# Four of the ten token-group norms of an adaLN block transposed by the DMA crossbar instead of TensorE

## The chip, the cores and the metric
The kernel runs on one core of one Trainium2 chip. The metric is the device time of one execution in microseconds; the median of ten runs of the kernel before is 248.68 us (247.54 to 251.53). A core has five engines with a queue each: TensorE (PE, matmuls; PEld is its weight load), VectorE (DVE), ScalarE (ACT), GpSimd (POOL) and SyncE (SP), which here only issues DMAs. The profile's lines name them so.

## The reference
One transformer block on 2048 tokens of width 512, in bf16. A conditioning vector gives six rows of 512: a shift, a scale and a gate for each half of the block.

```python
mod = (silu(c) @ w_mod).reshape(1, 6, 1, -1)
sa, ca, ga, sb, cb, gb = (mod[:, i] for i in range(6))
h = layernorm(x) * (1 + ca) + sa
x = x + ga * attention(h, wqkv, wo)       # 32 heads of 16; each token sees 8 keys, 2 apart, backwards
h = layernorm(x) * (1 + cb) + sb
x = x + gb * ((gelu(h @ w_gate) * (h @ w_up)) @ w_down)      # 512 -> 1792 -> 512
```

The attention is a sliding, dilated one: `idx = pos[:, None] - 2 * arange(8)`, and positions before the first token are masked.

## The kernel before
**Groups.** The tokens are worked in five groups (`GROUPS`, L256): groups 0 and 1 of 256 tokens, groups 2, 3 and 4 of 512. Each goes through the same stages, and the loop at L928 emits them: `ln1` (first norm), `emit_qkv`, `emit_attention` (which ends with the second norm), and `emit_ffn` for the group before.

**Norms.** The tokens lie on the partitions when a norm is taken. `norm` (L529) writes (x - mean) * rstd for 128 tokens on VectorE into a tile `xn` of [128 tokens, 2, 512], so a 512-token group has two such tiles (`half` 0 and 1). The matmuls that follow need the 512 features on the partitions. `transposed` (L551) does that: TensorE transposes blocks of 128x128 into PSUM tiles `tp` (16 for a group of 512 tokens), and `modulate` (L545) takes each block row of 128 features from PSUM on ScalarE, multiplies by 1 + scale and adds the shift (both one number per partition there), and writes `hT` (first norm) or `h2T` (second norm), laid out [128, 4 feature blocks `dt`, tokens]. Four modulations make a group.

**Matmuls.** `emit_qkv` (L646) reads `hT[g][:, dt, 0:n]` as the moving operand, `emit_ffn` (L888) reads `h2[g][:, dt, 0:n]`, gate and up in turn (`g_ps`, `u_ps`); four matmuls over `dt` fill one PSUM tile. ScalarE takes the gelu of the gate (L897) and copies up (L900), VectorE multiplies them (L901), and the down projection `y_ps` (L914) is added to x on VectorE (L922) and stored (L925). For the last 128 tokens, the down projection is cut in two column ranges (`cuts`, L905), so that the first part can be added and stored while the second is computed.

**Attention.** Products q times shifted k on VectorE (`pq`, L728) are folded on TensorE (`LT`, L740); a maximum on VectorE, one matmul that subtracts it (L770), exponentials on ScalarE (L777), their sum on TensorE (`ss`, L785), its inverse on ScalarE (L790), products with v on VectorE (`pv`, L806), a fold (`o_ps`, L825) and the output projection (`x_ps`, L850). v goes to DRAM (`scr`, L672) and comes back in a shifted layout (`vR`, L689).

**Order.** No loop order is kept. Every operation is put into a `Plan` with an engine, an estimated time and a priority (`PRI`, smaller goes first). `Plan.order` (L92) is a list scheduler: it takes the operation that can start earliest by these estimates (with an added `MARGIN` for an operation's engine), and the priority decides among equals. A DMA is estimated by its issue time on SP and by its bytes over a bandwidth, plus a fixed latency; `AHEAD` and `SKEW` shape that. The result is one fixed instruction order on each engine. Every engine executes its queue in order, so an instruction that waits holds all behind it on that engine. All DMAs but one small one are issued from SP's queue. The tags in `BUFS` (L196) tell how many buffers each tile has: two for `hT`, `h2T`, `xn1` and `xn2`, and in PSUM four for `psF` and two each for `psL` and `psB`; the `tp` tiles of second norms are in `psB`, those of first norms of groups 1 to 4 in `psF`.

Of the kernel before, what the change touches and what calls it, by code (L numbers as in the profile page):

```python
# [8 lines left out]
ACT = mybir.ActivationFunctionType  # L9
ALU = mybir.AluOpType  # L10
AX = mybir.AxisListType
F32 = mybir.dt.float32
BF16 = mybir.dt.bfloat16
# [171 lines left out]
class Engines:  # L185
    def __init__(self, nc, pl):
# [11 lines left out]
        ("e", 1), ("oT", 1), ("h2T", 2), ("gl", 3), ("ub", 3), ("hh", 8))  # L198
BLOCKS1 = ()
BLOCKS2 = ()  # L200
LNACT = (0, 1)
SECOND = ()
MERGE = (3, 4)
FMERGE = 0
PRI = {
        "mod0": -12.4,
        "ln1": (-1502.5, -1237, -338.7, -29.4, 227.5),
        "qkv": (-71.9, 355.8, 239.3, 407.9, 1355.7),
        "att": (60.2, 400.6, -1102.5, 575.4, 1925.6),
        "ffn": (1146.5, 2723.5, 3129, 2182.7, 1503.5),  # L210
        "glu": (-357.2, 325.4, -1793.4, 205.8, 1599.5),
        "mod": (-117, -108, -507.7),
        "wo": 1499.4,
        "wd": 1669.5,
        "scr": -3244.8,
        "vR": -3579.5,
        "warm": (5, 7, 0, 3),
        "load": {"wv": -995.5, "x1": -998.36, "x2": -989.51, "wm2": -981.48, "wo": -880.76, "x3": -990.01,
        "wm3": -882.56, "wm4": -988.97, "x4": -992.67, "Wg": -867.81, "Wu": -862.75, "wm5": -862.25, "Wd":
        -862.75},  # L220
}
Plan.MARGIN = {"pe": 0.33, "act": 0.29, "dve": 0.21, "pool": 0.16, "sp": -1.5}
Plan.AHEAD = 3.4
Plan.SKEW = 1.21
Plan.TURN = 0
# [3 lines left out]
def kernel(  # L229
# [13 lines left out]
    nc = tc.nc  # L243
    P = 128
# [37 lines left out]
    def act_us(n, ptr=0):  # L282
        return 0.055 + n * 0.833e-3 + 0.093 * ptr
# [267 lines left out]
    def transposed(xns, n, dst, off, p, seq, tags, split, lo=0):  # L551
        per = 2 if n == SG else 4
        for dtp in range(DT // per):
# [16 lines left out]
            for dd in range(per):  # L570
# [6 lines left out]
                else:  # L577
                    modulate(dst, lambda dd=dd, tp=tp: tp[:, dd, 0:n], dt, off, n, p, [tp], lo)

    def ln1(g, dst, p):  # L580
        xns = []
        tok0, n = GROUPS[g]
        for half in range(n // 256):
# [24 lines left out]
            for i in range(2):  # L608
                norm(tok + P * i, xn, i, Mean(mv), rstd, p)
        transposed(xns, n, dst, 0, p, "ln1", ("psL",) if g == 0 else ("psF", "psF"), g == 0)  # L610

# [16 lines left out]
    def emit_qkv(g):  # L628
# [10 lines left out]
        for step, (b, j) in enumerate(order):  # L639
# [3 lines left out]
            def mm(b, j, ps, jls, dts):  # L643
                whole = len(dts) == DT
                for jl, dt in [(jl, dt) for jl in jls for dt in dts]:
                    nc.tensor.matmul(ps[:, jl, :], lhsT=wqkv[b][:, dt, j + jl:D:4], rhs=hT[g][:, dt, 0:n],  # L646
                                     start=(dt == 0 and (jl == 0 or whole)),
                                     stop=(dt == DT - 1 and (jl == nj - 1 or whole)))
# [29 lines left out]
    def emit_attention(g):  # L678
# [155 lines left out]
        lo = tok0 % SG if FMERGE else 0  # L834
        h2[g] = h2[g - 1] if lo else T("h2T", [P, DT, SG], BF16, "h2T")
        xns = []
        for half in range(n // 256):
# [31 lines left out]
            for i in range(2):  # L869
                norm(tok0 + 256 * half + P * i, xn, i, sx, rstd, p2)  # L870
        transposed(xns, n, h2[g], 8, base + 12, "ln2", ("psB", "psB"), False, lo)

    def emit_ffn(g):
# [4 lines left out]
        for u in range(units):  # L878
            p = PRI["ffn"][g] + u
            gu = []  # L880
            for Wt in (Wg, Wu):
                ps = T("psF", [P, nf, n], F32, "g_ps" if Wt is Wg else "u_ps", "ffn")

                def mm(Wt=Wt, ps=ps, u=u):
                    for f in range(nf):
                        ft = u * nf + f
                        for dt in range(DT):
                            nc.tensor.matmul(ps[:, f, :], lhsT=Wt[:, dt, ft * P:(ft + 1) * P],  # L888
                                             rhs=h2[g][:, dt, 0:n], start=(dt == 0), stop=(dt == DT - 1))

# [12 lines left out]
        for c4 in range(n // P):  # L903
            gc = tok0 // P + c4
            cuts = ((0, 256), (256, D)) if gc == S // P - 1 else ((0, D),)  # L905
            for cut, (lo_d, hi_d) in enumerate(cuts):
# [21 lines left out]
    for g in range(NG):  # L928
        hT[g] = T("hT", [P, DT, GROUPS[g][1]], BF16, "hT")
        ln1(g, hT[g], PRI["ln1"][g])  # L930
# [46 lines left out]
```

## Time and profile before

| What | us |
|---|---|
| median of 10 runs | 248.68 (247.54 to 251.53) |
| the profiled execution's own time | 248.26 |
| its span, first to last instruction | 246.2 |
| TensorE busy | 236.9 |
| VectorE busy | 158.6 |
| ScalarE busy | 158.6 |
| 128 transposes on TensorE, their share of busy time | 11.4 |

The page divides the span in 40 slices of 6.2 us and prints the busy share of each engine in each as a digit (9 is 90% or more). Groups of instructions are listed as line, engine, operation, output and inputs, shape, count, then busy time and mean duration in ns, then how long the engine sat idle just before them and what ended that. A matmul's duration is longer than the distance to the next one, since they are pipelined; from a timeline, the distance between starts gives what one costs. In a timeline's line stand start and length in us, then the instructions merged in it.

### The profile page before, as it was taken

What the parts mean: (1) busy time and instruction counts of PE and PEld (TensorE: products, weight loads), DVE (VectorE), ACT (ScalarE), POOL (GpSimd) and SP (SyncE); (2) the same over time, 40 slices, a digit from 0 to 9 for tenths busy, and PEclk for the clock granted to TensorE, in tenths of its full rate; (3) what the DMA queues carried; (4) which work ended last, traced back from release to release, by engine and by line L of the source; (5) the groups of instructions that cost most, each with busy time, mean ns of one, the idle gap of its engine ahead of it and who ended that gap; (6) DMA issues with size and microseconds to landing.
All of it is one profiled execution on the core that took longest, in us unless ns stands there. A gap on an engine that the chain in (4) does not pass through costs nothing.

```text
span 246.2 us, 4292 instructions
## 1 busy us (share of the span) xinstructions
PE 236.9 (96%) x1642; PEld 130.9 (53%) x1666; DVE 158.6 (64%) x302; ACT 158.6 (64%) x293; POOL 19.3 (8%) x37
## 2 busy tenths in 40 slices
PE   7699989999999999999999999999999999999995
PEld 3588545557675547675444444444445444444453
DVE  4589869739998699972699895189464222222222
ACT  5197887989476778568777575655768701666400
POOL 6004330010001000040000002000011000000000
PEclk9999999999999999999999999999999999999999
DMA  5999999998800129500108600001000010100011
GB/s 159 352 356 340 304 271 360 216 315 208 176 0 0 43 70 249 121 0 4 43 18 203 128 0 0 24 21 43 0 4 1 0 42 3 43 0 0 3 43 43
DMA packets 27030, 25.89 MB, mean 105 GB/s; under 512 B 1409, under 2 KB 25858, under 8 KB 27010
## 3 DMA queue, kind: packets, MB, share of 16 engines
q1 hardware_dynamic: 27008, 25.61, 38.8%
q8 instruction: 13, 0.21, 0.4%
q14 instruction: 7, 0.06, 0.1%
q10 hardware_dynamic: 2, 0.00, 0.0%
HBM read 21.40 MB, written 4.21 MB: 104 GB/s over the span
## 4 chain that ended last, share of the span: by engine, by line
PE 79%; DVE 6%; DMA 5%; SPq 3%; ACT 2%; POOL 1%; issue 1%; DVEq 0%; POOLq 0%
PE u_ps L888 20%; PE g_ps L888 20%; PE y_ps L914 19%; PE qkv_ps L646 7%; PE x_ps L850 5%; DMA wm<-in_w_mod_dram 3%; DVE st L592 3%; PE o_ps L825 3%; PE LT L740 2%; DMA wk<-in_A_wqkv_dram 2%; PE tp L560 2%; POOL rstd L536 1%; DVE pq L728 1%; DVE xn L531 1%; SPq L414 1%
## 5 line engine op out<-in xcount | busy, mean ns | idle before, releaser
L888 PE MATMUL g_ps<-h2T,Wg 128*128 128x512 bf16 (+1 forms) x277 | 57.2, 336 | 0.2
L888 PE MATMUL u_ps<-h2T,Wu 128*128 128x512 bf16 (+1 forms) x275 | 57.1, 336 | 0.2
L914 PE MATMUL y_ps<-WdP,hht 128*128 128x512 bf16 (+1 forms) x231 | 50.6, 366 | 0.3
L897 ACT ACTIVATE gl<-g_ps 128x512 bf16<-128x512 f32 x56 | 33.7, 602 | 24.1 <-PE g_ps L888 16.3
L900 ACT CAST ub<-u_ps 128x512 bf16<-128x512 f32 x56 | 32.8, 586 | 17.5 <-PE u_ps L888 16.5
L901 DVE TENSOR_TENSOR hht<-gl,ub 128x512 bf16<-128x512 bf16 x56 | 23.4, 425 | 32.0 <-ACT ub L900 31.4
L888 PEld LDWEIGHTS <-Wu 128*128 128x128 bf16 x280 | 26.9, 98 | 22.4 <-issue 1.9
L888 PEld LDWEIGHTS <-Wg 128*128 128x128 bf16 x280 | 27.2, 98 | 21.4 <-issue 0.4
L728 DVE TENSOR_TENSOR pq<-qT,kT 128x2048 bf16<-128x2048 bf16 x32 | 37.9, 1222 | 0.3 <-ACT kT L668 0.3
L914 PEld LDWEIGHTS <-hht 128*128 128x128 bf16 x238 | 23.1, 98 | 23.9
L922 DVE TENSOR_TENSOR x_sg<-y_ps,x_sg 128x512 bf16<-128x512 f32 (+1 forms) x17 | 10.7, 656 | 28.6 <-PE y_ps L914 28.6
L806 DVE TENSOR_TENSOR pv<-e,vR 128x2048 bf16<-128x2048 bf16 x24 | 28.3, 1222 | 0.1
L536 POOL TENSOR_TENSOR rstd<-rstd,neghalf 128x2 f32<-128x2 f32 x14 | 15.0, 1076 | 166.5 <-DVE rstd L865 107.6
L646 PE MATMUL qkv_ps<-hT,wk 128*128 128x512 bf16 (+1 forms) x76 | 16.1, 335 | 0.8 <-DMA wk<-in_A_wqkv_dram 0.5
L646 PE MATMUL qkv_ps<-hT,wq 128*128 128x512 bf16 (+1 forms) x79 | 16.6, 336 | 0.1
L646 PE MATMUL qkv_ps<-hT,wv 128*128 128x512 bf16 (+1 forms) x80 | 15.7, 337 | 0.0
L850 PE MATMUL x_ps<-woP,oT 128*128 128x512 bf16 x61 | 15.0, 379 | 0.2
L546 ACT ACTIVATE h2T<-tp,modT,scl 128x512 bf16<-128x512 bf16 (+1 forms) x20 | 12.8, 695 | 2.2 <-PE tp L560 2.2
L857 ACT ACTIVATE xn<-x_sg 128x512 bf16<-128x512 bf16 x16 | 10.1, 629 | 4.8 <-DVE x_sg L854 4.5
L668 ACT CAST kT<-qkv_ps 128x512 bf16<-128x512 f32 x16 | 9.4, 589 | 4.6 <-PE qkv_ps L646 4.1
L668 ACT CAST qT<-qkv_ps 128x512 bf16<-128x512 f32 x16 | 9.5, 593 | 4.4 <-PE qkv_ps L646 4.4
L854 DVE SCALAR_TENSOR_TENSOR x_sg<-x_ps,x_sg 128x512 bf16<-128x512 f32 x16 | 10.8, 691 | 1.8 <-PE x_ps L850 1.7
(92 smaller groups left out, 223.1 us busy)
## 6 DMA issues: line engine op xcount, KB each, us to landing
vR<-scr SPq DMA_DIRECT2D x24, 260.0 KB, 5.0
vR<-scr SPq DMA_DIRECT2D x8, 264.0 KB, 9.8
wm<-in_w_mod_dram SPq DMA_DIRECT2D x8, 256.0 KB, 5.5
out_dram<-x_sg SPq DMA_DIRECT2D x15, 128.0 KB, 1.7
Wg<-in_B_w_gate_dram SPq DMA_DIRECT2D x2, 896.0 KB, 9.4
scr<-vT SPq DMA_DIRECT2D x7, 256.0 KB, 6.2
Wu<-in_B_w_up_dram SPq DMA_DIRECT2D x2, 896.0 KB, 12.6
WdP<-in_B_w_down_dram SPq DMA_DIRECT2D x2, 896.0 KB, 8.8
```

What stands on the lines that cost most here:

```text
L536: gp(0.75, lambda: nc.gpsimd.tensor_tensor(out=rstd[:], in0=rstd[:], in1=neghalf[:, 0:2], op=ALU.pow), r=[rstd, neghalf], w=[rstd], pri=p)
L546: act(act_us(n, 2), lambda: nc.scalar.activation(out=dst[:, dt, lo:lo + n], in_=src(), func=ACT.Identity, scale=scl[:, off // 2 + dt:off / ...
L646: nc.tensor.matmul(ps[:, jl, :], lhsT=wqkv[b][:, dt, j + jl:D:4], rhs=hT[g][:, dt, 0:n], start=(dt == 0 and (jl == 0 or whole)), stop=(dt ...
L668: act(act_us(SG), lambda dst=dst, ps=ps: nc.scalar.copy(out=dst(), in_=ps[:]), r=[ps], w=w, pri=p)
L728: dve(1.145, lambda j=j, wg=wg, no=no, t=pq[m]: nc.vector.tensor_tensor(out=t[:], in0=_ap(q[g][:, j, :], [[0, no], [1, n]]), in1=_ap(kT[:, ...
L806: dve(1.145, lambda jj=jj, jl=jl, wg=wg, t=pv[m]: nc.vector.tensor_tensor(out=t[:], in0=_ap(e[:, wg, :], [[0, 4], [1, n]]), in1=vR[g][jj][ ...
L850: nc.tensor.matmul(x1_ps[:], lhsT=oT[:, j, c4 * P:(c4 + 1) * P], rhs=woP[:, j, :], start=(j == 0), stop=(j == 3))
L888: nc.tensor.matmul(ps[:, f, :], lhsT=Wt[:, dt, ft * P:(ft + 1) * P], rhs=h2[g][:, dt, 0:n], start=(dt == 0), stop=(dt == DT - 1))
L897: act(act_us(SG), lambda gl=gl, ps=gu[0]: nc.scalar.activation(out=gl[:], in_=flat(ps), func=ACT.Gelu_apprx_tanh), r=[gu[0]], w=[gl], pri= ...
L900: act(act_us(SG), lambda ub=ub, ps=gu[1]: nc.scalar.copy(out=ub[:], in_=flat(ps)), r=[gu[1]], w=[ub], pri=p)
L901: dve(0.339, lambda gl=gl, ub=ub, ht=hh[u // 2], u=u: nc.vector.tensor_tensor(out=ht[:, u % 2, :], in0=gl[:], in1=ub[:], op=ALU.mult), r=[ ...
L914: nc.tensor.matmul(y_ps[:], lhsT=hh[u // 2][:, u % 2, f * n + c4 * P:f * n + (c4 + 1) * P], rhs=WdP[:, ft, lo_d:hi_d], start=(ft == 0), st ...
```

## The change
The second norms of groups 2, 3 and 4 and the first norm of group 4 no longer use `transposed`. A new helper `crossbar` issues one `dma_start_transpose` from SP for each of a group's two `xn` tiles (256 KB each, SBUF to SBUF), which writes the tile transposed into `hT` or `h2T`. Then four ScalarE instructions scale and shift that tile in place. These tiles are laid out [128, token block, feature block, 128 tokens], so the matmuls read their moving operand in four runs of 128 columns with a stride (`columns`), and write their PSUM tile under the same shape (`shaped`).

All priorities and load priorities are set anew, as are the margins, `AHEAD` and `SKEW`. The last 128 tokens' down projection is cut at column 384 instead of 256.

```diff
-BLOCKS1 = ()
-BLOCKS2 = ()
+CUT = 384
+XB1 = {4: "act"}
+XB2 = {2: "act", 3: "act", 4: "act"}
 PRI = {
-        "mod0": -12.4,
-        "ln1": (-1502.5, -1237, -338.7, -29.4, 227.5),
-        "qkv": (-71.9, 355.8, 239.3, 407.9, 1355.7),
-        "att": (60.2, 400.6, -1102.5, 575.4, 1925.6),
-        "ffn": (1146.5, 2723.5, 3129, 2182.7, 1503.5),
+        "mod0": -90.9,
+        "ln1": (-1628, -1309.8, -689.8, -49.3, 487.8),
+        "qkv": (-615.4, 221.2, 164.3, 607.2, 1344.9),
+        "att": (-458.5, 37.3, -1094.5, 559.4, 1849),
+        "ffn": (1261.5, 2894.6, 2852.9, 2242.7, 1657.1),
...
-        "load": {"wv": -995.5, "x1": -998.36, "x2": -989.51, "wm2": -981.48, "wo": -880.76, "x3": -990.01,
-        "wm3": -882.56, "wm4": -988.97, "x4": -992.67, "Wg": -867.81, "Wu": -862.75, "wm5": -862.25, "Wd":
+        "load": {"wv": -995.5, "x1": -998.36, "x2": -995.23, "wm2": -996.59, "wo": -880.76, "x3": -1009.12,
+        "wm3": -995, "wm4": -996.09, "x4": -995.73, "Wg": -870.11, "Wu": -862.75, "wm5": -860.91, "Wd":
         -862.75},
 }
-Plan.MARGIN = {"pe": 0.33, "act": 0.29, "dve": 0.21, "pool": 0.16, "sp": -1.5}
-Plan.AHEAD = 3.4
-Plan.SKEW = 1.21
+Plan.MARGIN = {"pe": 0.45, "act": 0.17, "dve": 0.22, "pool": 0.29, "sp": -0.46}
+Plan.AHEAD = 2.49
+Plan.SKEW = 2
...
+    def crossbar(xns, n, dst, off, p, on):
+        for half, xn in enumerate(xns):
+            dma(262e3, lambda half=half, xn=xn: nc.sync.dma_start_transpose(
+                out=dst[:, 2 * half:2 * half + 2, :, :].rearrange("p c d t -> p (c d) t"),
+                in_=xn[:].rearrange("p i d -> p (i d)")), r=[xn], w=[(dst, ("half", half))], pri=p, us=1.25, bw=290e3)
+        for dt in range(DT):
...
+                act(act_us(n, 2), lambda dt=dt: nc.scalar.activation(
+                    out=dst[:, :, dt, :], in_=dst[:, :, dt, :], func=ACT.Identity,
+                    scale=scl[:, off // 2 + dt:off // 2 + dt + 1], bias=modT[:, off + dt:off + dt + 1]),
+                    r=[dst, (scl, off), (modT, off)], w=[(dst, dt)], pri=p)
+
+    def columns(t, g, dt, xb):
+        return t[:, :, dt, :] if g in xb else t[:, dt, 0:GROUPS[g][1]]
+
+    def shaped(ap, g, xb):
+        return ap.rearrange("p (c t) -> p c t", t=P) if g in xb else ap
...
-        transposed(xns, n, dst, 0, p, "ln1", ("psL",) if g == 0 else ("psF", "psF"), g == 0)
+        if g in XB1:
+            crossbar(xns, n, dst, 0, p, XB1[g])
+        else:
+            transposed(xns, n, dst, 0, p, "ln1", ("psL",) if g == 0 else ("psF", "psF"), g == 0)
...
-                    nc.tensor.matmul(ps[:, jl, :], lhsT=wqkv[b][:, dt, j + jl:D:4], rhs=hT[g][:, dt, 0:n],
+                    nc.tensor.matmul(shaped(ps[:, jl, :], g, XB1), lhsT=wqkv[b][:, dt, j + jl:D:4],
+                                     rhs=columns(hT[g], g, dt, XB1),
...
-        transposed(xns, n, h2[g], 8, base + 12, "ln2", ("psB", "psB"), False, lo)
+        if g in XB2:
+            crossbar(xns, n, h2[g], 8, base + 12, XB2[g])
+        else:
+            transposed(xns, n, h2[g], 8, base + 12, "ln2", ("psB", "psB"), False, lo)
...
-                            nc.tensor.matmul(ps[:, f, :], lhsT=Wt[:, dt, ft * P:(ft + 1) * P],
-                                             rhs=h2[g][:, dt, 0:n], start=(dt == 0), stop=(dt == DT - 1))
+                            nc.tensor.matmul(shaped(ps[:, f, :], g, XB2), lhsT=Wt[:, dt, ft * P:(ft + 1) * P],
+                                             rhs=columns(h2[g], g, dt, XB2), start=(dt == 0), stop=(dt == DT - 1))
...
-            cuts = ((0, 256), (256, D)) if gc == S // P - 1 else ((0, D),)
+            cuts = ((0, CUT), (CUT, D)) if gc == S // P - 1 else ((0, D),)
```

## The prediction
> **What bounds the kernel now.** I read the page's busy shares and slices first, then the busy time by stage, the groups by form, and the timelines of TensorE, ScalarE and VectorE around one second norm.
>
> The busy shares and the slices of the page:
> ```profile
> PE 236.9 (96%) x1642; PEld 130.9 (53%) x1666; DVE 158.6 (64%) x302; ACT 158.6 (64%) x293; POOL 19.3 (8%) x37
> PE   7699989999999999999999999999999999999995
> PEclk9999999999999999999999999999999999999999
> DMA  5999999998800129500108600001000010100011
> ```
> TensorE is busy nearly everywhere, at full clock, while the DMA engines are full only up to about 60 us. The stages (length, then busy us and instructions of each engine, clock, DMA share, GB/s):
> ```profile
> 6.00:12.00 6.00, 3.96 (x64) 3.35 (x61) 3.68 (x10) 0.66 (x6) 0.00 (x0) 1.00 1.08 352
> 30.00:40.00 10.00, 8.77 (x41) 4.58 (x41) 8.07 (x19) 8.24 (x16) 2.35 (x2) 1.00 1.15 288
> 100.00:120.00 20.00, 19.95 (x163) 12.66 (x162) 12.17 (x32) 14.71 (x28) 3.02 (x2) 1.00 0.09 23
> 180.00:200.00 20.00, 19.89 (x104) 9.59 (x105) 7.88 (x25) 12.29 (x25) 1.38 (x2) 1.00 0.01 2
> 240.00:246.20 6.20, 3.22 (x25) 2.25 (x23) 1.45 (x3) 0.00 (x0) 0.00 (x0) 1.00 0.14 42
> ```
> Of 9.3 us in which TensorE is idle, 3.3 lie before 12 us (loads), 1.2 in 30 to 40 us, and 3.0 after the last matmul; from 60 to 240 us under 1 us is left. So the time is the sum of TensorE's work plus about 9 us, and work taken from TensorE after 40 us shortens the end one for one, as long as nothing new makes it wait.
>
> **The transposes removed.** Groups by form:
> ```profile
> L560 PE MATMUL tp<-ident,xn 128*128 128x128 bf16 x128 | 11.4, 219 | 0.1
> L546 ACT ACTIVATE h2T<-tp,modT,scl 128x512 bf16<-128x512 bf16 x12 | 8.7, 782 | 1.7 <-PE tp L560 1.7
> L888 PE MATMUL g_ps<-h2T,Wg 128*128 128x512 bf16 x165 | 42.6, 379 | 0.2
> L310 PE MATMUL qkv_ps<-ident 128*128 128x512 bf16 x4 | 1.0, 379 | 0.0
> ```
> A 512-token group has 4 x 4 = 16 transposes of 128x128. Three second norms and the last first norm make 64 of the 128. The 219 ns of one is its latency, not its price, because matmuls are pipelined. The price is the step to what follows on the engine, here in TensorE's timeline at group 2's second norm:
> ```profile
> 110.21 0.40 PE L560 MATMUL tp<-ident,xn 128*128 128x128 bf16 x4
> 110.45 1.04 PE L888 MATMUL u_ps<-h2T,Wu 128*128 128x256 bf16 x8
> 111.32 0.39 PE L560 MATMUL tp<-ident,xn 128*128 128x128 bf16 x4
> 111.54 1.03 PE L914 MATMUL y_ps<-WdP,hht 128*128 128x512 bf16 x3
> ...
> 114.15 4.48 PE L914 MATMUL y_ps<-WdP,hht 128*128 128x512 bf16 x20
> 118.47 0.59 PE L785 MATMUL ss<-e,F 128*128 128x512 bf16 x2
> 118.90 1.03 PE L888 MATMUL g_ps<-h2T,Wg 128*128 128x512 bf16 x4
> ```
> Four take 111.54 - 111.32 = 0.22 us, or 0.24 by the pair before: 57 ns each. 64 x 57 ns = **3.65 us**, all in stages where TensorE has no gap. The Trainium skill ("VectorE: DVE Perf Modes", section on the three transpose paths) gives 390 ns for a 128x128 on TensorE and 1309 ns on the DMA crossbar. By its figure 64 x 390 ns = 25 us would go; that is a single transpose from end to end, and this trace has them at 57 ns, so I take 3.65.
>
> **The matmuls that read the new layout.** Their moving operand now comes in four runs of 128 columns, 1 KB apart: 3 x 112 gate and up matmuls and 48 of the last group's qkv, 384 in all. The nearest row is the filler L310, whose operand is also walked in four runs of 128 (with step 0): 379 ns, as the dense ones. So I take 0; if it cost 10 ns each, 3.8 us would eat the gain. The reshaped PSUM output is contiguous as before.
>
> **The modulation.** 16 ScalarE instructions stay (12 for h2T, 4 for hT) but read SBUF, not PSUM. ScalarE's row that reads SBUF (the square, 629 ns) is within 50 ns of those that read PSUM (about 590), so within 16 x 0.05 = 0.8 us of ScalarE time, at 64% busy: 0 on the path. The transposes' PSUM tiles disappear from two buffer tags, which can only help.
>
> **The crossbar DMAs.** 8 of 256 KB are added to SP's queue; no DMA crossbar is in this trace. Nearest by size and shape on the same queue is vR<-scr:
> ```profile
> vR<-scr SPq DMA_DIRECT2D x24, 260.0 KB, 5.0
> scr<-vT SPq DMA_DIRECT2D x7, 256.0 KB, 6.2
> ```
> All 32 vR loads land in 3.6 to 10.6 us, median 5.3, and hold SP 0.62 us each (the planner books 1.25 us of SP for a crossbar DMA). Lower bound: "DMA: Bandwidth & Descriptors" (latency and other measured facts) has crossbar transposes at 261 GB/s with a non-contiguous middle dimension, so 262 KB / 261 GB/s = 1.0 us of transfer, and about 3 us with a fixed part. Upper bound: the 1309 ns above for each of eight blocks, 10.5 us per DMA and 21 us for both halves in series. I take 5.5 us from the norm's end to landing, by the vR row, as both rest on the same queue and engines; the ends go into the range.
>
> **Where that latency lies.** Before, the transposes began as the norm ended and gave ScalarE its first tile 0.4 us later. Now, group by group: the norm's end, the landing 5.5 us later, and four modulations of 0.72 us (half of a pair's 1.45 us). The timelines of VectorE and ScalarE at group 2:
> ```profile
> 109.62 0.74 DVE L531 TENSOR_SCALAR xn<-x_sg,sx,rstd 128x512 bf16<-128x512 bf16 x2 [0.58 <-POOL rstd L536]
> 115.38 1.28 ACT L260 ACT_TABLE_LOAD   x1
> 116.67 1.09 ACT L777 ACTIVATE e<-LT 128x512 bf16<-128x512 f32 x2
> ```
> - Group 2: norm ends 110.4, landing 115.9, h2T ready 118.8 if the modulations go ahead of the exponentials, 120.6 if behind (117.75 + 2.9). TensorE has by then only the last unit and down projections of group 1; it ran into group 2's gate at 118.90, and without the 1.8 us of transposes removed up to there (this group's and hT's) it would at 117.1. A wait of 1.7 to 3.5 us in the old order, down to 0 where VectorE does the norm ahead of the two products (1.22 us each) that lay between its steps at 104 to 107 us. I take **1.0**.
> - Group 3: norm ends 150.4, ready 158.8 to 160.7; gate matmuls at 161.67, less 2.7 us of transposes is 159.0, and 2.6 us of down projections of group 2 stand behind them (163.4 to 166.0) and can be put in between: 0. Without that cover, up to 1.7.
> - Group 4: norm ends 187.9, ready 196.3, first used at 202.5 - 3.6 = 198.9: hidden with 2.6 us left.
> - First norm of group 4: hT was ready at 46.5, its qkv began at 76; even a landing of 10.6 us is hidden. The DMA engines are full there, so 0.52 MB at 350 GB/s push the weights behind it back 1.5 us; gate work needs Wg from 57 us, but the last group's qkv (48 matmuls by 0.216 us, 10.4 us, run only from 76 us on) can stand in: 0.
>
> SP is in order: between 97 and 119 us it has nothing, at 149 the next is an output store that waits for a down projection, at 185 likewise; a crossbar DMA put behind such a store would be late by the store's wait (up to 6 us at 150), which the planner's due times avoid if its 1.25 us and 290 GB/s are about right. Behind a crossbar that waits for its norm stand only stores, for which nobody waits before the end, and near 40 us the vR loads and weights, which have the cover just named. POOL's queue is not touched.
>
> **New priorities and the tail.** The load order moves wm2 (524 KB, 1.5 us at 350 GB/s) ahead of wv, while TensorE already waits for loads before 12 us: 0 to +1.5 us; qkv of the second group is there to fill, so 0. The last down projection is cut at 384 instead of 256: the last VectorE add has 128 columns, about 0.28 us for 0.42, and its store 32 KB for 64: **-0.2 us**.
>
> **Sum**, against the profiled execution (248.26 us, of which 246.2 span): 248.26 - 3.65 - 0.2 + 1.0 = 245.4. It was 0.42 under the median of the runs (248.68), so **245.8 us** in the median, 1.2% faster. With TensorE's 390 ns of the page it would be about 224, with the page's crossbar price about 275 (below).
>
> **Rivals.** A measurement of this kernel tells about 0.3% (0.75 us) from no change.
> 1. My case, most of the transposes' time gained, a wait of about 1 us at group 2: 244.9 to 246.8. Chance 0.45.
> 2. All hidden, and the new order also takes some of the 5.0 us idle before 40 us: 248.68 - 3.85 - up to 2.5, 242.3 to 244.9. For it: DMA share is 0.09 at 100 to 120 us, so a crossbar DMA has the engines to itself. Against: the VectorE chain before group 2's norm doesn't shorten. Chance 0.25.
> 3. The wait equals the gain, 248.3: modulations behind the exponentials (3.5 us). Chance 0.1.
> 4. Slower: the crossbar is late at group 2. Ready time passes 117.1 + 3.85 = 120.95 once the landing comes more than 7.7 us after the norm, and from there it decides. At the vR row's worst, 10.6 us: landing 121.0, ready 123.9, wait 6.8: 248.68 - 3.85 + 6.8 = 251.6. At the page's 1309 ns per block: second half lands 108.3 + 21 = 129.3, ready 132.2, a wait of 15 at group 2, 9 at group 3, 6.6 at group 4: 275. For it: that row of the page; against: the same page would have TensorE at 390. Chance 0.2.
>
> So faster 0.71, within 0.3% 0.08, slower 0.21. The range, 242.8 to 250.2, leaves out the far ends of 2 and 4; the likeliest case alone is 244.9 to 246.8.
>
> **What would show it.** The transposes' group on TensorE at 64 instead of 128, and TensorE's instructions fewer by 64. Crossbar DMAs on SP landing in 4 to 7 us. No TensorE gap over 0.5 us except one before group 2's first gate matmul, put down to ScalarE's h2T. Gate matmuls on the new layout still at 379 ns and 0.216 us apart. It is wrong if the landing is over 8 us, if the step of the gate matmuls grows, or if the first 60 us show more idle TensorE than 5.5 us.

## The result, and the profile after
The changed kernel takes 246.74 us in the median of 15 runs (244.55 to 248.01), the kernel before 249.04 in the runs of the same chip (52 runs): a ratio of 0.9912, with an interval of 0.9891 to 0.9933. That is 2.3 us, or 0.9%, faster; 2.9 us were predicted. The profiled execution took 246.37 us, with a span of 244.3. A few executions of some kernels take over 1.5% more than the fastest of the same kernel; the ratios, and the sorting by clock below, leave them out.

From the page after, busy shares and slices:
```profile
PE 235.5 (96%) x1580; PEld 127.2 (52%) x1598; DVE 158.5 (65%) x302; ACT 159.1 (65%) x293; POOL 15.6 (6%) x37
PE   7899699999999999999999999999999999999994
PEclk9999799999999999999999999999999999999999
```
TensorE has 62 records fewer (64 were expected; a few can be missing), but its busy time fell by only 1.4 us, not by 3.65, and the fifth slice of the clock, full before, now has 7 tenths. The stages of after, with the same columns as before (length, busy us and instructions of TensorE, weight load, VectorE, ScalarE and GpSimd, then clock, DMA share, GB/s):
```profile
6.00:12.00 6.00, 5.34 (x73) 4.31 (x71) 3.68 (x10) 1.93 (x8) 0.00 (x0) 1.00 1.09 358
20.00:30.00 10.00, 7.77 (x106) 5.21 (x105) 9.94 (x34) 6.15 (x11) 2.97 (x4) 0.88 1.07 306
30.00:40.00 10.00, 9.85 (x56) 5.69 (x56) 6.23 (x11) 8.33 (x16) 1.34 (x2) 0.95 1.14 285
100.00:120.00 20.00, 19.95 (x154) 12.46 (x154) 11.71 (x31) 15.90 (x30) 1.48 (x2) 1.00 0.19 41
180.00:200.00 20.00, 19.89 (x92) 9.11 (x93) 8.52 (x27) 12.34 (x24) 1.38 (x2) 1.00 0.14 27
```
6 to 12 us got fuller (5.34 us of matmul for 3.96), and from 100 us on TensorE is as full as it was. The loss is between 20 and 40 us: more idle time and a clock of 0.88 and 0.95. Cut finer, this is the stretch:
```profile
27.00:28.00 1.00, 1.00 (x5) 0.45 (x4) 1.00 (x4) 0.87 (x2) 0.07 (x1) 0.76 0.97 369
28.00:30.00 2.00, 1.78 (x5) 0.66 (x5) 2.00 (x9) 0.58 (x1) 0.00 (x0) 0.50 1.12 222
30.00:31.00 1.00, 1.00 (x8) 0.84 (x7) 0.86 (x3) 0.72 (x2) 0.07 (x1) 0.53 1.16 139
```
0.24 + 2 x 0.50 + 0.47 = 1.7 us of clock are lost there. What lies ahead of it shows in TensorE's timeline, first of before, then of after (start, length, instructions; in brackets the idle time before and what ended it):
```profile
32.67 0.38 PE L770 MATMUL LT<-Lb,NB 128*128 128x512 bf16 x1 [1.18 <-DVE Lb L765]
```
```profile
24.27 0.61 PE L561 MATMUL tp<-ident,xn 128*128 128x128 bf16 x8
26.84 0.39 PE L798 MATMUL LT<-Lb,NB 128*128 128x512 bf16 x1 [1.96 <-DVE Lb L793]
27.07 1.47 PE L673 MATMUL qkv_ps<-hT,wq 128*128 128x512 bf16 x4
28.33 0.63 PE L673 MATMUL qkv_ps<-hT,wk 128*128 128x512 bf16 x1
```
TensorE waits 1.96 us (before: 1.18) for the maximum of group 0's scores, which VectorE makes in three steps, and soon after runs at half clock: the next query and key matmuls are 0.4 us apart instead of 0.22. VectorE's timeline of after says why the maximum is late:
```profile
25.06 0.28 DVE L789 TENSOR_TENSOR Lb<-Lb 128x256 bf16<-128x256 bf16 x1
...
25.32 0.23 DVE L624 TENSOR_SCALAR rstd<-mv 128x2 f32<-128x2 f32 x2
25.59 0.29 DVE L791 TENSOR_TENSOR Lb<-Lb 64x256 bf16<-64x256 bf16 x1
25.79 0.68 DVE L616 BATCH_NORM_STATS2 st<-x_sg 128x6 f32<-128x512 bf16 x1
26.51 0.28 DVE L793 TENSOR_TENSOR Lb<-Lb 32x256 bf16<-32x256 bf16 x1
```
The statistics of later groups' norms (0.68 us each) stand ahead of the three steps and between them; VectorE is busy 9.94 of 10 us here. None of it has to do with a crossbar, whose first DMA is issued at 50 us. It comes of the new order, as the first experiment confirms.

The crossbar's own lines, in the groups by form and in the DMA issues of after:
```profile
L919 PE MATMUL g_ps<-h2T,Wg 128*128 128x512 bf16 x168 | 43.1, 379 | 0.0
L593 ACT ACTIVATE h2T<-h2T,modT,scl 128x512 bf16<-128x512 bf16 x12 | 9.1, 809 | 1.7 <-DMA h2T<-xn 1.7
L561 PE MATMUL tp<-ident,xn 128*128 128x128 bf16 x64 | 5.6, 225 | 0.0
L593 ACT ACTIVATE hT<-hT,modT,scl 128x512 bf16<-128x512 bf16 x4 | 3.0, 812 | 2.4 <-DMA hT<-xn 2.4
```
```profile
h2T<-xn SPq DMA_TRANSPOSE x6, 3.0
hT<-xn SPq DMA_TRANSPOSE x2, 7.5
```
64 transposes are left, gate matmuls on the strided tile last 379 ns as before, and a crossbar DMA lands in 3.0 us where the DMA engines are free (7.5 where they are full). And group 2's gate, where a wait was forecast, in TensorE's and in ScalarE's timeline of after:
```profile
117.83 1.03 PE L945 MATMUL y_ps<-WdP,hht 128*128 128x512 bf16 x4
118.70 1.03 PE L919 MATMUL g_ps<-h2T,Wg 128*128 128x512 bf16 x4
```
```profile
112.53 0.81 ACT L593 ACTIVATE h2T<-h2T,modT,scl 128x512 bf16<-128x512 bf16 x1
113.36 1.28 ACT L261 ACT_TABLE_LOAD   x1
114.65 1.08 ACT L805 ACTIVATE e<-LT 128x512 bf16<-128x512 f32 x2
115.62 2.21 ACT L593 ACTIVATE h2T<-h2T,modT,scl 128x512 bf16<-128x512 bf16 x3
```
There is no wait: the gate follows its neighbours at the usual step, with h2T ready at 117.8.

The span's balance, from the busy time of both profiled executions by stretch: transposes -3.65 us by the prediction's price; idle time before 20 us from 3.35 to 2.19, -1.16; idle time in 20 to 40 us from 1.60 to 2.38, +0.78; clock there +1.7; idle time in 60 to 80 us +0.35 (a subtraction at 76.85 us that waits for VectorE's maximum); idle time in other stretches -0.47. The sum is -2.4, and the span went from 246.2 to 244.3, by 1.9: some 0.5 us are not placed. This is the account of one execution each. It does not say what the kernel would gain if the slow clock went away, since another wait may take its place; the experiments show that one does.

### The profile page after: what moved, and what is told of

It reads as the page before. It is cut to its first block, busy times and chain, and to the rows that moved or that the text cites. A ratio compares the mean times of both kernels' runs of the same rounds, so it can differ in the third digit from the quotient of the medians.

```text
span 244.3 us, 4191 instructions
## 1 busy us (share of the span) xinstructions
PE 235.5 (96%) x1580; PEld 127.2 (52%) x1598; DVE 158.5 (65%) x302; ACT 159.1 (65%) x293; POOL 15.6 (6%) x37
## 2 busy tenths in 40 slices
DMA packets 35477, 27.97 MB, mean 114 GB/s; under 512 B 9985, under 2 KB 34306, under 8 KB 35458
## 4 chain that ended last, share of the span: by engine, by line
PE 76%; DVE 8%; DMA 6%; ACT 3%; SPq 3%; issue 2%; POOL 1%; DVEq 0%; POOLq 0%
PE y_ps L945 18%; PE u_ps L919 18%; PE g_ps L919 17%; PE qkv_ps L673 11%; PE x_ps L878 5%; DMA hT<-xn 3%; PE o_ps L853 3%; DMA wk<-in_A_wqkv_dram 2%; DVE st L616 2%; PE LT L768 2%; DVE pq L756 2%; ACT hT L547 1%; SPq L717 1%; PE LT L798 1%; SPq L415 1%
## 5 line engine op out<-in xcount | busy, mean ns | idle before, releaser
L919 PE MATMUL u_ps<-h2T,Wu 128*128 128x512 bf16 (+1 forms) x280 | 57.7, 337 | 0.0
L945 PE MATMUL y_ps<-WdP,hht 128*128 128x512 bf16 (+2 forms) x230 | 49.9, 366 | 0.5 <-issue 0.2
L953 DVE TENSOR_TENSOR x_sg<-y_ps,x_sg 128x512 bf16<-128x512 f32 (+2 forms) x17 | 10.9, 658 | 27.3 <-PE y_ps L945 27.3
L537 POOL TENSOR_TENSOR rstd<-rstd,neghalf 128x2 f32<-128x2 f32 x14 | 11.3, 814 | 170.6 <-DVE rstd L893 108.1
L673 PE MATMUL qkv_ps<-hT,wk 128*128 128x512 bf16 (+1 forms) x78 | 16.8, 346 | 0.3 <-issue 0.2
L673 PE MATMUL qkv_ps<-hT,wv 128*128 128x512 bf16 (+1 forms) x79 | 15.2, 337 | 0.3 <-DMA wv<-in_A_wqkv_dram 0.2
L616 DVE BATCH_NORM_STATS2 st<-x_sg 128x6 f32<-128x512 bf16 x16 | 10.4, 682 | 2.7 <-DMA x_sg<-in_A_x_dram 2.7
L673 PEld LDWEIGHTS <-wk 128*128 128x128 bf16 x80 | 8.7, 116 | 5.5 <-issue 1.5
```

The source lines that it names most:

```text
L537: gp(0.75, lambda: nc.gpsimd.tensor_tensor(out=rstd[:], in0=rstd[:], in1=neghalf[:, 0:2], op=ALU.pow), r=[rstd, neghalf], w=[rstd], pri=p)
L616: dve(0.6, lambda i=i, st=st, tok=tok: nc.vector.bn_stats(out=st[:, i, :], in_=xrow(tok + P * i)), r=[xkey(tok + P * i)], w=[(st, i)], pri=p)
L673: nc.tensor.matmul(shaped(ps[:, jl, :], g, XB1), lhsT=wqkv[b][:, dt, j + jl:D:4], rhs=columns(hT[g], g, dt, XB1), start=(dt == 0 and (jl = ...
L919: nc.tensor.matmul(shaped(ps[:, f, :], g, XB2), lhsT=Wt[:, dt, ft * P:(ft + 1) * P], rhs=columns(h2[g], g, dt, XB2), start=(dt == 0), stop ...
L945: nc.tensor.matmul(y_ps[:], lhsT=hh[u // 2][:, u % 2, f * n + c4 * P:f * n + (c4 + 1) * P], rhs=WdP[:, ft, lo_d:hi_d], start=(ft == 0), st ...
```

## The experiments
Theory A: the crossbar DMAs gain nearly all of the transposes' 3.65 us, and what is missing was spent by the new order, on the idle time at 25 us and the clock behind it. Rivals: B, the new order is itself a gain and the crossbar brings less than 3.65; C, the crossbar is hidden by so little that it decides the time, as the prediction's fourth case had it. All times are medians, each with its ratio to the kernel before measured beside it (248.76 to 249.06 us). No kernel leaves work out.

**The new order without the crossbar.** All transposes on TensorE, all else as in the changed kernel.
```diff
-XB1 = {4: "act"}
-XB2 = {2: "act", 3: "act", 4: "act"}
+XB1 = {}
+XB2 = {}
```


> The new order alone: the changed kernel's priorities, margins, load order and tail cut, with all transposes on TensorE as before. If the gain comes from the transposes and the new order by itself costs (idle of 2.0 us near 25 us and 1.7 us of slow clock after it, less 1.1 us gained before 20 us), it is 246.7 + 3.65 = 250.4, slower than the kernel before by 1.4. If the new order is what gains, it is 246.7 to 247.5.


Measured: 249.98 us, ratio 1.0043 (1.0021 to 1.0065). The new order alone is 0.9 us slower than the old one, and its trace has the same gap (1.97 us, ended by the same maximum) and the same clocks, 0.88 in 20 to 30 us and 0.95 in 30 to 40. From here to the changed kernel it is 3.1 to 3.2 us: that is what the four crossbar norms are worth under these priorities, of 3.65. The scheduler places all else anew, so the two orders aren't the same instruction by instruction: ScalarE here swaps its function table ten times for eight, but TensorE waits nowhere for that (it is busy 20.00 of 20 us in each stretch from 60 to 240 us). That the new order is a gain, the first half of B, is out.

**One norm less.** The first norm of group 4 back on TensorE.
```diff
-XB1 = {4: "act"}
+XB1 = {}
```


> Only the second norms by crossbar; the last group's first norm is transposed by TensorE again. If each 16 transposes are worth 0.9 us, 246.7 + 0.9 = 247.6. If that crossbar DMA costs more than it saves, since it runs while the DMA engines are full with weights (landing 6.8 and 8.3 us in the trace), it is 246.7 or less.


Measured: 247.64 us, ratio 0.9954 (0.9933 to 0.9975): 0.75 to 0.9 us more than the changed kernel in its two measurements, and 16 x 57 ns are 0.91. The intervals only touch (0.9933 is in both), so this is barely clear of noise; it fits a transpose that is worth its 57-ns step, and excludes one of several hundred ns.

**The crossbar without the new order.** The old priorities, margins, load order and cut, and the scheduler free to place the new operations.
```diff
-CUT = 384
+CUT = 256
 PRI = {
-        "mod0": -90.9,
+        "mod0": -12.4,
...
-Plan.AHEAD = 2.49
-Plan.SKEW = 2
+Plan.AHEAD = 3.4
+Plan.SKEW = 1.21
```


> The crossbar alone: the changed kernel with the priorities, margins, load order and tail cut of the kernel before. If the gain is TensorE's 64 transposes by 57 ns (3.65 us), and the crossbar's latency is hidden, it is 249.0 - 3.65 = 245.4, granted clock 1.000, no TensorE gap at 25 us. If the order written for the crossbar is what hides it, a TensorE wait for ScalarE's h2T before group 2's first gate matmul of 1 to 3.5 us shows, and 246.5 to 249.


Measured: 263.45 us, ratio 1.0547 (1.0479 to 1.0616), 14 us slower; both expectations missed it. Its trace at group 2, TensorE first and then ScalarE:
```profile
123.49 1.46 PE L919 MATMUL g_ps<-h2T,Wg 128*128 128x256 bf16 x8 [2.23 <-ACT gl L928]
127.20 1.87 PE L919 MATMUL u_ps<-h2T,Wu 128*128 128x256 bf16 x8 [2.25 <-ACT ub L931]
```
```profile
118.45 1.28 ACT L261 ACT_TABLE_LOAD   x1
119.75 1.09 ACT L805 ACTIVATE e<-LT 128x512 bf16<-128x512 f32 x2
120.72 0.81 ACT L593 ACTIVATE h2T<-h2T,modT,scl 128x512 bf16<-128x512 bf16 x1
121.55 1.28 ACT L928 ACT_TABLE_LOAD   x1
...
124.16 1.28 ACT L261 ACT_TABLE_LOAD   x1
...
127.17 1.28 ACT L928 ACT_TABLE_LOAD   x1
```
ScalarE swaps its function table four times in 10 us, between exponential and gelu, with modulations between; 12 such loads in the whole run where the kernel before has 8. TensorE also runs 25 filler matmuls (`o_ps<-ident`, 5.7 us, in two blocks at 89 to 96 us), which the program writes where its estimates leave that engine without work. The run is so late because the same numbers, given other operations, made another order; how the 14 us divide over the causes was not settled. It is no measure of the crossbar's cost, so the next two keep the order.

**The old queues kept exactly.** Every engine's old order, with the transposes taken out of TensorE's queue, the crossbar DMA on SP in the place of the first of them, and ScalarE's modulations where they were (old numbers and cut as above).
```diff
+                def trans(half=half, dtp=dtp, xn=xn):
+                    if dtp == 0:
+                        nc.sync.dma_start_transpose(
...
+                pe(0.115 * per, trans, r=[xn, ident], w=[(tp, half), (dst, ("home", 0))], pri=p)
+            for dd in range(per):
+                act(act_us(n, 2), lambda dt=per * dtp + dd: nc.scalar.activation(
```


> The four crossbar transposes put into the kernel before with every other instruction at its old place: on TensorE the 64 transposes are left out, on SP a crossbar DMA stands where a tile's first transposes were issued, ScalarE's modulations keep their places and work in SBUF. If the latency is hidden where nobody uses the tile soon, it is 249.0 - 3.65 = 245.4 plus 1.5 of wait at group 2. If a modulation that waits for its DMA holds the PSUM copies behind it on ScalarE, the last group's first norm costs most: its modulations stood at 41.8 us, while the DMA engines are full and a crossbar DMA takes 7 us or more to land, so ScalarE and then TensorE stand some 6 us, and it is about 254.


Measured: 259.84 us, ratio 1.0442 (1.0399 to 1.0486), slower still than the 254 of the case that came true. Two lines, of ScalarE's and TensorE's timeline, hold most of it:
```profile
52.24 1.52 ACT L594 ACTIVATE hT<-hT,modT,scl 128x512 bf16<-128x512 bf16 x2 [10.24 <-DMA hT<-xn]
```
```profile
54.76 3.60 PE L879 MATMUL x_ps<-woP,oT 128*128 128x512 bf16 x8 [9.69 <-ACT oT L860]
```
The tile `hT` is first read at 66.3 us, and yet its lateness stops TensorE from 45 us on: SP reaches the two DMAs at 44.9 us, behind value loads and stores; ScalarE waits for them at the head of its queue, and behind it stand the copies of `oT`, which the output projection needs. From 50 to 58 us, at the end of that wait and behind it, the clock is 0.50.

**The same, second norms alone.** As the last, with group 4's first norm on TensorE.
```diff
-XB1 = {4: "act"}
+XB1 = {}
```


> The same with the second norms alone; the last first norm stays on TensorE. 48 transposes by 57 ns are 2.74 us. If the 3.0 us to landing is hidden in the old places, 249.0 - 2.7 = 246.3. If the modulations, which stand ahead of the exponentials and of PSUM copies on ScalarE, pass their wait on, about 1.6 us is lost at group 2, 1.2 at group 3 and 0.5 at group 4, and it is about 249.6.


Measured: 248.28 us, ratio 0.9969 (0.9945 to 0.9994), between the two expectations: 0.75 us gained of 48 x 57 ns = 2.74. Its ScalarE timeline at group 4, and what TensorE shows of it:
```profile
190.91 1.52 ACT L594 ACTIVATE h2T<-h2T,modT,scl 128x512 bf16<-128x512 bf16 x2 [1.26 <-DMA h2T<-xn]
```
```profile
192.96 1.02 PE L920 MATMUL g_ps<-h2T,Wg 128*128 128x512 bf16 x4 [0.53 <-ACT gl L929]
...
195.33 7.93 PE L946 MATMUL y_ps<-WdP,hht 128*128 128x512 bf16 x36 [0.48 <-ACT gl L929]
```
Again the wait is not for the modulated tile. It is for a gelu of another group that stands behind the waiting modulation.

**How late may it be?** In the changed kernel, the second half of each second norm's crossbar is issued twice, and then three times, to the same place: each repeat puts the landing about 3 us later, so about 6 and 9 us after the norm's end instead of 3.
```diff
+                for i in range(2 if off == 8 and half == 1 else 1):
+                    nc.sync.dma_start_transpose(
```


> The changed kernel with the second half's crossbar DMA of each second norm issued twice, one after the other, so that h2T lands some 3.1 us later; no other queue changes. By the changed kernel's trace the lateness reaches TensorE through ScalarE (the modulations and the exponentials behind them): about 1.3 us at group 2, 0.8 at group 3, 0 to 0.5 at group 4, so 246.8 + 2.3 = 249.1, and the gain is gone at 6.2 us from norm to landing. By the prediction's own point, 7.7 us from norm to landing, half of the gain should be left: 247.5.


Measured: 248.3 us, ratio 0.9981 (0.9962 to 0.9999), 1.4 to 1.6 us over the changed kernel; the 249.1 that counted on ScalarE passing its wait on was too high, the 247.5 by the prediction's point too low.
```diff
+                for i in range(3 if off == 8 and half == 1 else 1):
+                    nc.sync.dma_start_transpose(
```


> The same with three issues: h2T lands some 6.2 us later than in the changed kernel, 9.3 us after its norm. If ScalarE passes all further lateness on, at group 2 and 3 another 3 us each and at group 4 about 3: 249.1 + 9 = 258. If only TensorE's reading of h2T counts and the output projections stand in at groups 3 and 4, about 3 us more than with two issues: 252.


Measured: 259.84 us, ratio 1.0442 (1.0394 to 1.049), 13 us over the changed kernel, near the 258 expected if ScalarE passes all lateness on. With two issues, ScalarE waits 1.96, 4.92 and 3.50 us for the landings, and TensorE only 0.21 us at group 2's gate, 0.30 and 0.17 us at score sums. With three, TensorE waits at group 2 like this:
```profile
120.56 1.07 PE L817 MATMUL ss<-e,F 128*128 128x512 bf16 x2 [2.83 <-ACT e L809]
121.43 1.91 PE L949 MATMUL y_ps<-WdP,hht 128*128 128x512 bf16 x4
123.13 1.68 PE L923 MATMUL g_ps<-h2T,Wg 128*128 128x512 bf16 x4
```
It is stopped first by the exponentials, which stand behind the first modulation on ScalarE, and the four gate matmuls then take 1.68 us for 1.03, at half clock. The waits of 2.8, 3.4 and 2.7 us (groups 2, 3 and 4), with a slow stretch behind the first two, are where the 13 us begin. So a landing 3 us later costs about 1.5 us, and one 6 us later 13: the cliff of C is there, but the changed kernel stands back from it.

**Filling the gap.** Eight matmuls of the identity into a PSUM tile that nobody reads, ahead of group 0's subtraction, so that TensorE isn't idle while it waits.
```diff
         def sub_max():
+            if g == 0:
+                for i in range(8):
+                    nc.tensor.matmul(gap[:], lhsT=ident[:], rhs=_ap(ident[:], [[0, 4], [1, P]]), start=True, stop=True)
```


> Eight matmuls of the identity, into a PSUM tile that nobody reads, ahead of the first group's subtraction of the maximum, where TensorE of the changed kernel idles 1.96 us (24.9 to 26.8 us); nothing else differs in the order on any engine. If the slow clock at 27 to 31 us comes of that idle time, the granted clock is 1.000 and the time 246.7 - 1.7 = 245.0, though no useful work is moved. If the clock falls for another reason (the mix of matmuls, the DMA load, chance), it stays at 0.993 and the time at 246.7 or a little above.


Measured: 245.92 us, ratio 0.9886 (0.9844 to 0.9927), and a mean granted clock of 0.993 in five of the six runs: neither the 1.000 nor the 245.0 came. The windows of its profiled run:
```profile
6.00:12.00 6.00, 4.61 (x60) 3.38 (x59) 3.67 (x10) 0.65 (x5) 0.00 (x0) 0.76 1.04 339
27.00:31.00 4.00, 3.76 (x22) 1.86 (x21) 3.94 (x15) 3.46 (x6) 1.44 (x2) 1.00 1.14 249
```
In this execution the clock behind the gap is whole, but it is slow for 3.4 us from 9.1 us on, behind waits for loads, where the changed kernel's first profile had 1.00.

**Filling both.** The same, and four more such matmuls at 7 to 8 us, ahead of the second part of the modulation's columns.
```diff
             def cols(n=n, mps=mps, src=src[i2], gap0=gap0):
+                for i in range(4 if gap0 is not None else 0):
+                    nc.tensor.matmul(gap0[:], lhsT=ident[:], rhs=_ap(ident[:], [[0, 4], [1, P]]), start=True, stop=True)
```


> The changed kernel with the gap at 25 us filled by eight matmuls of the identity, and the wait for w_mod at 7 to 8 us by four more. Nothing else differs in any queue. If the two slow stretches of the clock (at 27 to 31 us in the changed kernel, at 8 to 12 us in the kernel with one gap filled) come of these idle times, the granted clock is 1.000 in most runs and the time 244.5 to 245.3. If they don't, the clock stays at 0.993 and the time at 245.9 or, by the added matmuls, above.


Measured: 245.92 us, ratio 0.9878 (0.9828 to 0.9927), and a mean granted clock of 0.998 or more in all six runs, as expected; the time is not (244.5 to 245.3 were). The runs lie from 244.44 to 247.33. The profiled one is the longest. VectorE's timeline, and TensorE's behind it, show a load in the place of the slow clock:
```profile
38.13 4.63 DVE L849 TENSOR_TENSOR pv<-e,vR 128x2048 bf16<-128x2048 bf16 x4 [4.24 <-DMA vR<-scr]
```
```profile
41.68 0.40 PE L862 MATMUL o_ps<-pv,F 128*32 128x256 bf16 x8 [0.47 <-DVE pv L849]
42.82 0.40 PE L862 MATMUL o_ps<-pv,F 128*32 128x256 bf16 x8 [0.73 <-DVE pv L849]
```
The same instruction in the changed kernel and in the kernel before:
```profile
36.70 4.63 DVE L840 TENSOR_TENSOR pv<-e,vR 128x2048 bf16<-128x2048 bf16 x4 [1.95 <-DMA vR<-scr]
36.83 4.63 DVE L812 TENSOR_TENSOR pv<-e,vR 128x2048 bf16<-128x2048 bf16 x4
```
With the clock mended, the next bound near 40 us is the shifted values' way through DRAM. The other profiles agree. Of the new order's profiled executions, the two without a slow stretch ahead of 40 us (this one, and the one with three issues) have TensorE idle for 1.5 and 1.4 us in 40 to 60 us; those with one or two (the changed kernel twice, all transposes on TensorE, two issues, one norm less, one gap filled) have 0 to 0.3 us. So most of the 1.7 us that a slow stretch takes lies in the shadow of the value loads.

**The changed kernel once more**, for its spread.

> The changed kernel itself, beside the others on the same chip: 246.7, granted clock 0.993 or 0.986 in most runs.


Measured: 246.89 us, ratio 0.9918 (0.9894 to 0.9942). With the first measurement and its profiled execution, 37 runs can be sorted by the mean granted clock: 13 at 0.984 to 0.986 have a median of 247.82 us, 19 at about 0.993 246.37, and 5 at 0.998 or above 245.88 (244.55 to 248.01). A loss of 1.7 us is 0.7% of the span, so these should be runs with two slow stretches, with one and with none. By the medians the first stretch then costs 0.5 us and the second 1.45, not 1.7 each. This measurement's profile has both: 0.72 in 6 to 12 us, and half clock from 29.2 to 32.6 us, behind the same gap (1.97 us). The first of the two begins at 8.7 us, behind gaps of 0.6 and 0.4 us only; the 16 query matmuls there take 3.45 us, for 1.92 in the first profile:
```profile
7.86 0.35 PE L503 MATMUL modT_ps<-scT,wm 128*128 128x1 bf16 x8 [0.61 <-DMA wm<-in_w_mod_dram]
8.62 0.26 PE L503 MATMUL modT_ps<-scT,wm 128*128 128x1 bf16 x4 [0.41 <-DMA wm<-in_w_mod_dram]
...
8.90 3.45 PE L673 MATMUL qkv_ps<-hT,wq 128*128 128x256 bf16 x16
```

**A milder order.** The new order with a later priority for the modulation's columns and two other margins, to take the norm work from ahead of the maximum.
```diff
-        "mod": (-156.3, -280.2, 267.6),
+        "mod": (-156.3, -63.5, 267.6),
...
-Plan.MARGIN = {"pe": 0.45, "act": 0.17, "dve": 0.22, "pool": 0.29, "sp": -0.46}
+Plan.MARGIN = {"pe": 0.45, "act": 0.27, "dve": 0.22, "pool": 0.29, "sp": -0.41}
```


> The changed kernel with three of its ordering numbers moved (priority of the second norm's shift and scale columns, ScalarE's and SP's margins), chosen so that less of TensorE's work runs out before the first group's maximum near 25 us; the crossbars keep their places after 100 us. If the new order's cost is the idle stretch at 25 us and the slow clock after it, a stretch shorter by 0.7 us or so and no slow clock give 244.3 to 245.5. If a gap of over 1 us is left and still slows the clock, it is 246 to 246.7, as the changed kernel.


Measured: 247.41 us, ratio 0.9942 (0.9918 to 0.9965): a miss of both expectations. The gap shrank to 1.40 us only, waits of 0.67 and 0.73 us came in at 42 to 43 us, for the products with v, and the clock is slow at 9.3 to 12.7 us (0.77 in 6 to 12 us), though not behind the gap.

**That order with fillers** (five ahead of the subtraction, four at 7 to 8 us).
```diff
+                for i in range(5):
+                    nc.tensor.matmul(gap[:], lhsT=ident[:], rhs=_ap(ident[:], [[0, 4], [1, P]]), start=True, stop=True)
```


> The same with what idle time is left filled by matmuls of the identity, five ahead of the first group's subtraction of the maximum and four ahead of the first scale and shift columns. If idle time is what slows the clock: 1.000 in nearly all runs and 244.0 to 245.3. If it isn't, 0.993 and no better than without the filling.


Measured: 246.29 us, ratio 0.9899 (0.9876 to 0.9922). The clock came out as expected (0.999 or more in 11 of 12 runs), the time didn't: 0.21 and 0.73 us of the value wait remain. No version is shown to be faster than the changed kernel: the best two medians, 245.92, have intervals that reach over its own.

Of theory A, then, two parts are shown: the crossbar norms bring 3.1 to 3.2 us, and the new order alone costs 0.9. That filled gaps keep the clock whole is shown by counting runs: 6 of 6 and 11 of 12 at 0.998 or above, for 5 of 37 and 5 of 12 without filling. That the gap and the clock are all of the 0.9 is not shown, as the value loads stand right behind them.

## Why the prediction was right, and where not
The direction held, and the size roughly: 245.8 predicted, 246.74 measured, just within the likeliest case's own 244.9 to 246.8 (246.89 the second time, just outside). But the likeliest case was not what happened: its wait at group 2 (+1.0) didn't come, and a loss of like size (+0.9) that the sum had at 0 came in its place. That the two nearly cancel is luck.

**Transposes, 57 ns each: right.** 16 of them put back cost 0.75 to 0.9 us, all 64 cost 3.1 to 3.2. The missing half microsecond of 3.65 was not settled; one candidate is the 0.35-us wait at 76.85 us (traced below), which the new order without the crossbar and the kernel with 16 transposes back do not show. The 390 ns that the Trainium skill has for a transpose ("VectorE: DVE Perf Modes", the three transpose paths) would have asked for 16 x 390 ns = 6.2 us in the first of these; taking the step from the timeline decided it.

**Strided operand: right.** 168 gate matmuls at 379 ns, 0.216 us apart.

**Modulation in place: right on the path, off in size.** An instruction takes 809 ns for 782, so 16 x 0.027 = 0.4 us of ScalarE's time, which nothing waits for.

**The crossbar's landing: 3.1 us, not 5.5.** The vR row was the wrong neighbour. Those loads mostly run while the DMA engines are full, and the crossbar DMAs of the second norms run alone. The two that do run in the crowd, at 50 to 56 us, take 6.8 and 8.3; the second is past the 8 us that was to show the prediction wrong. The estimate from the 1309 ns that the skill has for a 128x128 block on the crossbar ("VectorE: DVE Perf Modes", the three transpose paths), times the eight blocks of a DMA, is out: 10.5 us would have been past the cliff. The prediction's lower bound, about 3 us, is what came.

**Group 2's wait: 0, not 1.0.** The norm's second half ends at 108.4 us (110.4 before), since one product of VectorE instead of two lies ahead of it; landing 111.5, h2T ready at 117.8. The gate starts at 118.70, not at the 117.1 that the sum supposed, because the first 40 us gave 1.3 us back. Groups 3 and 4 were hidden as forecast: norm end to first modulation 3.5 us at group 3, and 4.5 us between the last modulation and the gate at group 4.

**The tail: 0, not -0.2.** From TensorE's last end to the span's end it is 2.9 us before and 3.0 after. The narrower last add does end sooner (0.33 us behind TensorE's last matmul, for 0.46), but VectorE's last three adds now come back to back (1.40 us), SP issues their stores in a row (1.30 us), and the last store is issued 0.2 us behind its add.

**The step that failed: "0 to +1.5 us; qkv of the second group is there to fill, so 0"**, for the new priorities. What it named as the risk, the loads before 12 us, went the other way: idle time before 20 us fell by 1.2 us. The cost lay in a place that it never looked at: VectorE's queue at 25 us, though 1.2 us of the idle time that it counted in 30 to 40 us lay at this very subtraction (the 1.18 us at 32.67 us, ended by the same maximum). The new order alone measures +0.9 in the medians, where 0 was booked. In the profiled executions it is 0.8 us more idle time in 20 to 40 us and 1.7 us of clock, less the 1.2. How the 0.9 divides is open: the order also reaches the products with v before their loads, which the kernel before doesn't wait for, and an execution that keeps its clock waits there instead. The forecast's condition "more idle TensorE than 5.5 us in the first 60 us" did not trip (4.7 us); it counted idle time and not the clock. Its sign "no TensorE gap over 0.5 us" elsewhere did, at 1.96 us.

Behind this stands a rule of the skill ("TensorE: Matmul & The Clock Gate", Part 1): the clock falls to half after an idle window of about 3.4 us, counted in windows that run freely, and comes back after a busy one. Read as a rule about one gap, it lets a wait of 1.96 us cost only itself; here the wait was followed by a loss of 1.7 us of clock in four of the six profiled executions that have it, and by nothing in the other two. The slow stretch's own length, 3.4 us, agrees with the rule's window. Nor does the length of the gap decide: gaps of 0.6 and 0.4 us were enough at 8.7 us. Both places have in common that TensorE does only narrow work for longer than the gap: from 22.6 to 26.8 us it runs only transposes and matmuls of 1 or 16 columns besides the wait, and in the second profile from 6.0 to 8.9 us only transposes and matmuls of one column. Whether the clock counts such work as idle was not tested; wide matmuls put into both places kept it whole.

**A right result on a wrong reason: "first norm of group 4 hidden", because its qkv began at 76 us.** That is a misreading: in the kernel before, four query matmuls of this group read hT at 55.2 us, 8.7 us after it was ready; the rest come from 76 us on. And keeping the old queues shows even that cover to be worth nothing: the waiting modulation blocks ScalarE for 10 us, and what stands behind it is needed at once. In the changed kernel it is hidden, but for some tenths, because the order moved these four modulations from 41.8 to 64.2 us and the first reader to 81.6 us. ScalarE still waits 2.35 us for the DMA there, and the chain that ended last runs from that landing (8.3 us) through ScalarE and VectorE to the 0.35-us wait at 76.85 us; in the second profile, where both land in 6.8 us, it doesn't. For second norms, too, the old order gives 0.75 us of 2.74. So the new order costs 0.9 us and is what makes 3.1 us possible; the prediction had the two as separate terms.

**The rival on the slow side** (decides beyond 7.7 us from norm to landing): not refuted. The point lies between the two landings that were tried, 6 us, which took 1.5 us of the gain, and 9 us, which cost 13. But the place and the size were wrong: it let the gate wait for h2T, which at 9.3 us would cost 1.6 us, while the late runs wait for exponentials and gelus behind the modulation.

A smaller reading was off without effect: TensorE of before is idle for 1.04 us from 60 to 240 us, not under 1.

## What to carry to other kernels
When an operation moves from a busy engine to a DMA, look at the in-order queue of the engine that consumes the result: the instruction that waits must stand where everything behind it can wait too, and it is not enough that its own reader comes late. Price an edit's "new priorities" as a change of their own: run the new order without the new operation, and the new operation without the new order (with every queue kept by hand where a scheduler places the instructions). A wait of TensorE can cost clock besides: here 1.7 us behind a wait of 2, in four profiled executions of six, and a handful of matmuls whose result nobody reads prevented that. But look at what bounds the stretch next before counting it as a gain: here the value loads took most of it back.

## What the runs showed of the hardware
- A 1.96-us idle stretch of TensorE was followed by about 3.4 us at half clock in four of six profiled executions, starting 0.7 to 1.2 us after work resumed; idle stretches of 1.18 us (kernel before) and 1.40 us (milder order) were not, in the one execution of each that was profiled. But gaps of 0.6 and 0.4 us among matmuls of one column were followed by the same 3.4 us at 8.7 us (changed kernel, second profile), and not in its first profile, where they were 0.2 and 0.4, or in that of the kernel before, where they were 0.6 and 0.4. The same instruction order ran with none, one or two such stretches.
- A crossbar DMA of 256 KB, SBUF to SBUF, takes 1.25 us of SP and lands 3.0 to 3.1 us after its issue when alone; between loads that fill the DMA engines it took 1.3 to 3.2 us of SP and landed after 6.8 to 8.3. Packets under 512 bytes rose from 1409 to 9985 with eight of them, some 1070 each, so they move in pieces of about 250 bytes.
- The kernel before, too, has a mean clock of about 0.993 in nearly half of its runs (59 of 124 in four measurements), 249.03 us in the median against 248.58 in those at 0.998 or above. Where its slow stretch lies was not traced; the same loss of clock costs the changed kernel about as much once (246.37 against 245.88), and 1.45 us the second time.
